# Spreading projection blocks over more steps of a two-branch attention kernel, and issuing its row transfers on two queues

## The chip, the cores and the metric

One core of one Trainium2 chip. The metric is device time in microseconds (us), the median of three runs. Engines: PE is TensorE, DVE is VectorE, ACT is ScalarE, POOL is GpSimd, SP is SyncE, which here only issues DMAs.

## What is computed

Two full self-attentions with weights of their own over the same input `x` of 2048 x 640, 32 heads of 20 features each, mixed by a gate per row. The input `B_x` takes no part.

```python
def attention(x, wqkv, wo):                      # for A and for B
    qkv = (x @ wqkv).reshape(B, S, 3, H, Dh).transpose(2, 0, 3, 1, 4)
    q, k, v = qkv[0], qkv[1], qkv[2]
    scores = einsum("bhqd,bhkd->bhqk", q, k) * Dh ** -0.5
    o = einsum("bhqk,bhkd->bhqd", softmax(scores), v)
    return o.transpose(0, 2, 1, 3).reshape(B, S, D) @ wo

g = sigmoid((x * gate_w).sum(-1, keepdims=True))
return g * attention(x, A_wqkv, A_wo) + (1 - g) * attention(x, B_wqkv, B_wo)
```

## The kernel before

The 64 heads of A and B are taken in 16 groups of four. A group's work is 4 row blocks of 512 queries, and each row block is 8 **steps** of 256 keys: 512 steps in all, numbered G, 32 to a group. "Step 5 of a group" counts from the group's first step, 0. The loop over G (L1121) writes the whole program in Python, engine by engine, before anything runs; the order on each engine is then fixed.

In every step stand

- the scores of the step: 8 products of 128 keys x 512 queries (`scores`, L631), each followed by an exponential on ACT (L642);
- the value products (`values`, L652) of the step before, which add into one bank, `acc`;
- 8 products for the row maxima (`max_mm`, L560) of a unit 14 or 15 steps ahead, each followed by a maximum over 512 keys on DVE (L587). In two of eight the pair goes another way, a relu on ACT (L580) and one operation of DVE (L584) that adds and takes the maximum at once. The first steps have up to 12 such products;
- none, one or two **blocks** of projection work (`X` in the lists `STEP`, L45). A block is a run of about 15 products (`mms`, L370) that fills a third of a chunk of Q and K features (`project_a`), of the rest of the Q features (`project_r`), a tile of V (`project_v`), or a part of the output projection (`products`, L710, and `last_tiles`, L820); then ACT drains it (L404, L532, L722).

An **empty** step has no block, a **single** one block, a **double** two. Score products use half of the rows of the TensorE array each, so the two heads of a pair run side by side. All these products and blocks write to a ring of seven PSUM banks.

Which blocks run where is planned in the list `fill`, with entries of a release step, a due step, a number of blocks and a generator (L1006, L1019, L1026). `behind` (L1062) adds up what is due; the loop (L1133) writes two blocks where `behind` says so, one where anything has been released, none otherwise. Other tasks are put at fixed steps with `at` and `tasks`: the load and split of the weights of the next groups (`weights_a`, `weights_r`, `weights_v`), the latter with a maximum and a scale on DVE (L511 to L513).

A projected chunk of Q and K lies in a tile `cq` (two halves of 1024 columns, each with a buffer), with features as rows. Before a group can use it, its rows must be **spread** (`spread`, L428) to the two pairs of heads in the tiles `kt` and `qt`, by 18 DMAs per half, and 4 for the differences of keys (`kd`, L469). Each `rows` call (L419) issues two DMAs, L423 and L425. In the steps all are issued by SP; in the start, before step 0, SP and POOL take turns. `later` (L485) waits for the second step of the group before and for the rest rows, then issues both halves, one DMA each time that the generators are advanced, eight times in a step. `spread_done` holds the halves that are out; maxima of a group are not written before its halves are in it.

After a unit's maxima are complete, `finish_max` (L591) transposes them, POOL casts them to `m4r`, and SP sends them through DRAM into rows of `qt` (L613, L617). At the end of a row block `take_acc` (L739) drains `acc`, makes the reciprocal sums with DVE and POOL (`sq`, `sh`) and sends the normalised rows to DRAM.

Of the kernel before, what the change touches and what calls it, by code (L numbers as in the profile page):

```python
# [24 lines left out]
NT = S // P  # L25
NC = D // P
GH = 4
NG = H // GH
GF = GH * DH
QB = 512  # L30
NQ = S // QB
NS = 8
STEPS = 2 * NG * NQ * NS
LEAD = 15
VW = DH + 1
XE = 7
QKS = 2.0 ** -12
# [25 lines left out]
def kernel(  # L63
# [10 lines left out]
    nc = tc.nc  # L74
# [47 lines left out]
    now = [-1]  # L122
# [153 lines left out]
    side = []  # L276
# [43 lines left out]
    spread_done = set()  # L320
    r_done, v_done = set(), set()
    rk = {}
# [26 lines left out]
    def rest_tiles(i):  # L349
        rk[i] = wts.tile([P, 2, S], F16, name="rk", tag="rk", bufs=1)  # L350

    def weights_r(i):

        st = {}

        def load():
            t = st["t"] = wts.tile([P, NC, 160], F32, name="wstage", tag="wstage", bufs=2)
            w = wqkv[i // 2].rearrange("(c p) f -> p c f", p=P)
            for j in range(4):
                f = (4 * (i % 2) + j) * GF + 48  # L360
                nc.sync.dma_start(t[:, :, 32 * j:32 * j + 32], w[:, :, f:f + 32])

        def split():
            hi, lo = blk["r", i] = block_tiles("r")
            rest_tiles(i)
            split_weights(st["t"][:, :, :P], r_qk[i][:, 0:1], hi, lo)

        return load, split
# [77 lines left out]
                yield from rows(qt[:, 1, cols], base, 8 * (1 - j), rk[g // 4][f, :, cols], 12 + 8 * j, False, queues)  # L446

    def project_r(i, ch):
        n = slice(ch * QB, (ch + 1) * QB)
        yield from project_chunk(blk["r", i], rk[i][:, 0, n], rk[i][:, 1, n], ch)  # L450
        r_done.add((i, ch))
# [24 lines left out]
    def project_a(g, ch):  # L476
        if ch % 2 == 0:
            half_tiles(g)
        hl = blk["q", g]
        n = slice((ch % 2) * QB, (ch % 2 + 1) * QB)  # L480
        yield from project_chunk(blk["a", g], hl[:, 0, n], hl[:, 1, n], ch)
        if ch == 1:
            key_differences(g, hl, work.tile([P, QB], F32, name="fs"), work.tile([P, 2, QB], F16, name="dd", bufs=1))
        if ch % 2 == 1:
            def later():  # L485
                for _ in range(10):
                    yield
                while not {(g // 4, c) for c in (ch - 1, ch)} <= r_done or now[0] < (g - 1) * NQ * NS + 1:
                    yield
                if ch == 1:  # L490
                    yield from spread_differences(g)
                yield from spread(g, hl, ch // 2 * 1024, 1024)
                spread_done.add((g, ch // 2))

            side.append(later())
# [494 lines left out]
    def at(G, f):  # L990
        todo.setdefault(G, []).append(f)

    def soon(due, blocks, gen):

        fill.append((0, due, blocks, gen))

    def tasks(G, gap, fs):
        for k, f in enumerate(fs):
            at(G + k * gap, f)

    at(4, sigmoids)
    for g in range(2 * NG):
        b = g * NQ * NS
        n = g + 1
        if n < 2 * NG:
            fill += [(b - 8, b + 4 + ch, 3, project_a(n, ch)) for ch in range(4)]  # L1006
            if n + 1 < 2 * NG:
                tasks(b + 15, 3, weights_a(n + 1))
            i = g // 4 + 1
            if i < 4:  # L1010
                if g % 4 == 0:
                    z, c0 = i // 2, 320 * (i % 2)
                    parts = max_tasks([[(wqkv[z], part * D + c0 + 160 * k) for k in range(2)] for part in range(2)],
                                      lambda m, i=i: scales_qk(i, m))
                    tasks(b + 2, 2, parts)
                if g % 4 == 2:
                    tasks(b + 18, 3, weights_r(i))
                if g % 4 == 3:
                    fill += [(b - 9, b + 4 + ch, 3, project_r(i, ch)) for ch in range(4)]  # L1019
# [51 lines left out]
    def slot(G):  # L1071
        if not current:
            able = [f for f in fill if f[0] <= G]
            if not able:
                return
            first = min(able, key=lambda f: f[1])
# [44 lines left out]
    for G in range(STEPS + 1):  # L1121
        g, qb, i = unit_of(G)
        now[0] = G
        while G < STEPS and ((g, qb) not in ready or (G and not valued(G - 1))):
            for u, ch in next_maxima(G, 1):
                for j in (1, 0):
                    one_max(u, ch, j)
            finish_step()
            advance()
            product()  # L1130
            slot(G)
        some = next_maxima(G, 4)
        blocks = 0 if not current and not any(f[0] <= G for f in fill) else 2 if behind(G) else 1  # L1133
        count = {}
        for what in (STEP[blocks] if maxima or some else LATE + " X" * (blocks == 2)).split():
            k = count[what] = count.get(what, 0) + 1
            if what[0] == "e":
                q = sum(count.get(f"e{j}", 0) for j in range(2)) - 1
                j = int(what[1])
                if G < STEPS:  # L1140
                    scores(G, (k - 1) // 2, (k - 1) % 2, (j,))
                finish_step()
                advance()
                if q == 3:
                    for f in todo.pop(G, []):
                        f()
                    out_tasks(G)
            elif what[0] == "m":
                for u, ch in some[(k - 1) * len(some) // 4:k * len(some) // 4]:
                    one_max(u, ch, int(what[1]))  # L1150
            elif what == "V":
                product()
                if G:
                    values(G - 1, k - 1)
                    if G % NS == 0 and k == 2 and G < STEPS:
                        side.append(take_acc(*unit_of(G - 1)[:2]))
                        advance()
            else:
                slot(G)
# [35 lines left out]
```

## Time and profile before

| | us |
|---|---|
| median of 3 runs (lowest, highest) | 2866.06 (2865.85, 2867.37) |
| the profiled execution | 2865.34 |
| its span, first to last instruction | 2863.5 |
| first exponential of step 0 | 97.7 |
| PE, ACT, DVE, POOL busy | 2805.2, 2567.4, 2405.1, 678.5 |

A row of a group names line, engine, operation, what is written from what, and the count; then the busy time and the mean in ns of one; then the idle time of the engine ahead of them and what ended most of it. A row of a stretch names its begin and end in us from the span's start, its length, each engine's busy time with the number of instructions in it, the granted clock as a share, the DMA engines' busy share and GB/s. In rows of one line's DMAs, `SPq` are the issues by SP, with the time of an issue as lowest/median/highest in ns. A wait row names who waited, for whom, the sum in us, how often, and the longest. PE's busy time counts products that overlap, so that it is near 100% whether or not PE is the limit; the length of a stretch says more.

### The profile page before, as it was taken

What the parts mean: (1) busy time and instruction counts of PE and PEld (TensorE: products, weight loads), DVE (VectorE), ACT (ScalarE), POOL (GpSimd) and SP (SyncE); (2) the same over time, 40 slices, a digit from 0 to 9 for tenths busy, and PEclk for the clock granted to TensorE, in tenths of its full rate; (3) what the DMA queues carried; (4) which work ended last, traced back from release to release, by engine and by line L of the source; (5) the groups of instructions that cost most, each with busy time, mean ns of one, the idle gap of its engine ahead of it and who ended that gap; (6) DMA issues with size and microseconds to landing.
All of it is one profiled execution on the core that took longest, in us unless ns stands there. A gap on an engine that the chain in (4) does not pass through costs nothing.

```text
span 2863.5 us, 63124 instructions
## 1 busy us (share of the span) xinstructions
PE 2805.2 (98%) x23489; PEld 982.2 (34%) x23489; DVE 2405.1 (84%) x4637; ACT 2567.4 (90%) x5249; POOL 678.5 (24%) x1103
## 2 busy tenths in 40 slices
PE   6999999999999999999999999999999999999998
PEld 3533223342323323343233333334433333332222
DVE  6688898878898898978988888887788888889982
ACT  3799999989999999989999999998899999888987
POOL 5322113221221212233431111322112233120011
PEclk9999999999999999999999999999999999999999
DMA  4110101001020101202022020210202112221222
GB/s 134 41 38 6 37 10 41 15 15 31 14 52 17 31 15 27 50 10 52 18 45 53 14 60 16 47 37 21 47 21 54 44 35 66 62 72 52 69 61 74
DMA packets 176761, 114.77 MB, mean 40 GB/s; under 512 B 111812, under 2 KB 150396, under 8 KB 176452
## 3 DMA queue, kind: packets, MB, share of 16 engines
q1 hardware_dynamic: 173908, 109.12, 15.9%
q8 instruction: 184, 3.01, 0.4%
q0 software_dynamic: 1600, 0.96, 0.2%
q14 instruction: 125, 1.02, 0.1%
q10 hardware_dynamic: 944, 0.66, 0.1%
HBM read 48.89 MB, written 26.61 MB: 26 GB/s over the span
## 4 chain that ended last, share of the span: by engine, by line
PE 91%; DVE 3%; ACT 2%; DMA 1%; issue 1%; POOL 1%; SPq 0%; POOLq 0%; ACTq 0%; DVEq 0%
PE acc L657 34%; PE bank L639 19%; PE bank L377 19%; PE bank L576 17%; DVE mpart L587 2%; ACT pt L642 1%; PE bank L763 1%; ACT rl L580 1%; PE bank L600 0%; DMA xs<-in_A_x_dram 0%; DMA wv<-in_A_wqkv_dram 0%; DVE rl L584 0%; PE bank L185 0%; ACT ot L742 0%; PE bank L880 0%
## 5 line engine op out<-in xcount | busy, mean ns | idle before, releaser
L642 ACT ACTIVATE pt<-bank 128x512 f32<-128x512 f32 x4096 | 2179.1, 613 | 154.5 <-PE bank L639 85.6
L587 DVE TENSOR_REDUCE mpart<-bank 128x1 f32<-128x512 f32 x2976 | 1883.8, 684 | 337.4 <-PE bank L576 202.8
L657 PE MATMUL acc<-pt,v 128*21 128x512 f32 x8192 | 1081.8, 600 | 2.5 <-ACT ot L742 2.4
L639 PE MATMUL bank<-qt,kt 64*128 64x512 f16 x4096 | 1054.7, 380 | 7.2 <-ACT pt L642 2.9
L576 PE MATMUL bank<-kt,qt 60*128 60x512 f16 x3536 | 1011.0, 380 | 4.6 <-DVE mpart L584 0.9
L576 PEld LDWEIGHTS <-qt 60*128 60x128 f16 x4096 | 235.2, 94 | 679.3 <-issue 621.6
L639 PEld LDWEIGHTS <-kt 64*128 64x128 f16 x4096 | 248.8, 94 | 461.6 <-issue 329.1
L584 DVE CUSTOM_DVE_ANT_0 rl<-bank,rl 128x512 f32<-128x512 f32 x560 | 378.6, 680 | 23.0 <-PE bank L576 9.2
L580 ACT ACTIVATE rl<-bank 128x512 f32<-128x512 f32 x560 | 332.8, 600 | 13.7 <-PE bank L576 11.4
L377 PE MATMUL bank<-xx,wbh 128*128 128x168 f16 (+2 forms) x2240 | 280.0, 244 | 4.5 <-ACT xx L884 1.9
L657 PEld LDWEIGHTS acc<-pt,v 128*21 128x21 f32 x8192 | 143.1, 99 | 403.8 <-issue 384.3
L377 PE MATMUL bank<-xx,wbl 128*128 128x168 f16 (+2 forms) x1120 | 253.0, 243 | 0.0
L768 POOL CAST on<-ot 128x512 f16<-128x512 f32 x63 | 38.5, 611 | 822.6 <-DVE ot L765 796.0
L377 PEld LDWEIGHTS <-wbh 128*128 128x128 f16 x2240 | 184.2, 98 | 87.4 <-issue 80.5
L576 PE MATMUL bank<-kd,qt 60*128 60x512 f16 x560 | 203.5, 381 | 1.6 <-DMA kd<-dd 1.2
L377 PE MATMUL bank<-wvh,xx 128*128 128x160 f16 (+1 forms) x1280 | 155.4, 234 | 0.5 <-ACT rl L580 0.2
L377 PE MATMUL bank<-woh,o_in 128*128 128x160 f16 (+1 forms) x960 | 155.7, 256 | 0.0
L377 PEld LDWEIGHTS <-xx 128*128 128x128 f16 x1920 | 131.9, 97 | 52.2 <-issue 49.0
L377 PE MATMUL bank<-wvl,xx 128*128 128x160 f16 (+1 forms) x640 | 137.3, 231 | 0.6 <-POOL wvl L317 0.6
L608 POOL CAST m4r<-mt 16x128 f16<-16x128 f32 x128 | 33.4, 284 | 437.8 <-ACT mt L605 437.8
L377 PEld LDWEIGHTS <-o_in 128*128 128x128 f16 (+1 forms) x1440 | 104.0, 97 | 75.3 <-issue 62.0
L404 ACT ACTIVATE fs<-bank 128x168 f32<-128x168 f32 (+1 forms) x216 | 69.3, 321 | 52.4 <-PE bank L377 38.7
(137 smaller groups left out, 1395.5 us busy)
## 6 DMA issues: line engine op xcount, KB each, us to landing
y_scr<-y_out SPq DMA_DIRECT2D x32, 320.0 KB
kt<-cq SPq DMA_DIRECT2D x120, 80.0 KB
o_scr<-on SPq DMA_DIRECT2D x240, 40.0 KB
kt<-cq SPq DMA_DIRECT2D x136, 40.0 KB
xs<-in_A_x_dram SPq DMA_DIRECT2D x8, 640.0 KB
o_in<-o_scr SPq DMA_DIRECT2D x32, 160.0 KB
y_out<-y_scr SPq DMA_DIRECT2D x16, 320.0 KB
xx<-y_scr SPq DMA_DIRECT2D x16, 320.0 KB
```

Of the source, the lines that this page charges most:

```text
L377: nc.tensor.matmul(out_ap, a, b, start=(k == 0), stop=(k == len(pairs) - 1))
L404: nc.scalar.activation(f[:, m], pt[:, m], AF.Copy, scale=QKS)
L576: nc.tensor.matmul(pt, QT[g % 2][r, pair, q0:q0 + P], k, start=True, stop=True)
L580: nc.scalar.activation(relus[u, j], pt, AF.Relu)
L584: nc.vector.tensor_tensor_reduce(rl, pt, rl, 1.0, LOW, OP.add, OP.max, m)
L587: nc.vector.tensor_reduce(m, pt, axis=AX.X, op=OP.max)
L608: nc.gpsimd.tensor_copy(m4[:, k, :], mt)
L639: nc.tensor.matmul(et, KT[g % 2][r, pair, kt * P:(kt + 1) * P], QT[g % 2][r, pair, qb * QB:(qb + 1) * QB], start=True, stop=True)
L642: nc.scalar.activation(pt, et, AF.Exp, scale=factor(g // 4))
L657: nc.tensor.matmul(acc[32 * h:32 * h + VW, :], V[(g // 2) % 2][:, kt, (g % 2) * GH + h, :], ptiles.pop((G, kk, h)), start=(kt == 0), stop= ...
L763: nc.tensor.matmul(pt, sel.rearrange("k h e -> k (h e)"), sr, start=True, stop=True)
L768: nc.gpsimd.tensor_copy(o[:, 0], ot)
```

## The change

Blocks: `blocks_of` takes the place of the rule "two if behind, else one". A credit grows by `MEAN`, 0.72 a step in A's half and 1.1 in B's, and is spent by the blocks written; a step gets one when the credit has reached 1 or when the work would be behind at a rate of 0.8 blocks a step, and two when it is behind at a rate of 1. The release and due steps of all projections are moved, and weights are loaded and split earlier: `weights_a` by 3 steps, `weights_r` by 2, `weights_v` by 8 (but for the first). The tile of the rest rows, `rk`, is taken at its first block, not with its weights. Blocks of Q and K carry a fifth entry, and may not begin before that half of the group before has been spread.

Rows: in the steps, SP and POOL now take turns in a spread, so L423 stays with SP and L425 goes to POOL. The second half waits for step 8 of the group before instead of step 1, and for the first half.

```diff
+MEAN = (0.72, 1.1)
...
     def project_r(i, ch):
+        if i not in rk:
+            rest_tiles(i)
...
             def later():
+                two = cycle((nc.sync, nc.gpsimd))
                 for _ in range(10):
                     yield
-                while not {(g // 4, c) for c in (ch - 1, ch)} <= r_done or now[0] < (g - 1) * NQ * NS + 1:
+                while (not {(g // 4, c) for c in (ch - 1, ch)} <= r_done or now[0] < (g - 1) * NQ * NS + (1, 8)[ch // 2]
+                       or ch == 3 and (g, 0) not in spread_done):
                     yield
                 if ch == 1:
-                    yield from spread_differences(g)
-                yield from spread(g, hl, ch // 2 * 1024, 1024)
+                    yield from spread_differences(g, two)
+                yield from spread(g, hl, ch // 2 * 1024, 1024, queues=two)
...
+    def able(G):
+        return [f for f in fill if f[0] <= G and (f[4] is None or f[4][0] == 0 or f[4] in spread_done)]
...
-            fill += [(b - 8, b + 4 + ch, 3, project_a(n, ch)) for ch in range(4)]
+            fill += [(b - 13, b + (1, 3, 6, 8)[ch] + 3 * (g % 4 == 3), 3, project_a(n, ch), (n - 1, ch // 2)) for ch in range(4)]
             if n + 1 < 2 * NG:
-                tasks(b + 15, 3, weights_a(n + 1))
+                tasks(b + 12, 3, weights_a(n + 1))
...
                 if g % 4 == 2:
-                    tasks(b + 18, 3, weights_r(i))
+                    tasks(b + 16, 3, weights_r(i))
                 if g % 4 == 3:
-                    fill += [(b - 9, b + 4 + ch, 3, project_r(i, ch)) for ch in range(4)]
+                    fill += [(b - 12, b + 2 * ch, 3, project_r(i, ch), (g, 1)) for ch in range(4)]
...
-                at(b, load)
-                at(b + 3, lambda scale=scale: side.append(scale()))
-                at(b + 7, split)
-                fill += [(b + 10, b + 14 + 3 * j, 2, project_v(gg, j)) for j in range(0, NT, 2)]
+                b0 = b - 8 if g else b
+                at(b0, load)
+                at(b0 + 3, lambda scale=scale: side.append(scale()))
+                at(b0 + 7, split)
+                fill += [(b0 + 10, b0 + 18 + 2.9 * j, 2, project_v(gg, j), None) for j in range(0, NT, 2)]
...
-    def behind(G):
+    def behind(G, rate):
         n = sum(f[0] for f in current)
-        for f in sorted((f for f in fill if f[0] <= G), key=lambda f: f[1]):
+        for f in sorted(able(G), key=lambda f: f[1]):
             n += f[2]
-            if n > max(1, f[1] - G):
+            if n > max(1, rate * (f[1] - G)):
                 return True
         return False
+    credit = [0.0]
+    def blocks_of(G):
+        if not current and not able(G):
+            return 0
+        credit[0] = min(max(credit[0], -1.0) + MEAN[G >= NG * NQ * NS], 2.0)
+        n = 2 if behind(G, 1.0) else max(int(behind(G, 0.8)), int(max(credit[0], 0.0)))
+        credit[0] -= n
+        return n
...
-        blocks = 0 if not current and not any(f[0] <= G for f in fill) else 2 if behind(G) else 1
+        blocks = blocks_of(G)
```

The lines of the kernel after stand up to nineteen further down than those before; L580, L642 and L532 of before are L584, L646 and L536, and L404 is L404 in both.

ACT's order shows the blocks best, since each has one drain. In group 1, at the step that begins with 42, ACT before has exponentials and a relu only:

```order
L642 ACTIVATE pt<-bank_93 128x512
L642 ACTIVATE pt<-bank_89 128x512
L642 ACTIVATE pt<-bank_92 128x512
L580 ACTIVATE rl<-bank_90 128x512
L642 ACTIVATE pt<-bank_94 128x512
```

At the same place after, the drain of a V tile has come in between:

```order
L646 ACTIVATE pt<-bank_89 128x512
L646 ACTIVATE pt<-bank_90 128x512
L536 ACTIVATE v_87<-bank_94 128x8x20
L646 ACTIVATE pt<-bank_91 128x512
L584 ACTIVATE rl<-bank_89 128x512
```

A block of V has moved into an empty step; steps 40 and 43 got one too, and 41 stays empty. In group 2, where step 89 begins, ACT before drains two blocks of a chunk, the end of one step's and the beginning of the next's:

```order
L642 ACTIVATE pt<-bank_94 128x512
L642 ACTIVATE pt<-bank_89 128x512
L404 ACTIVATE fs<-bank_90 128x168
L404 ACTIVATE fs<-bank_91 128x168
L580 ACTIVATE rl<-bank_92 128x512
L642 ACTIVATE pt<-bank_93 128x512
```

After, it drains one:

```order
L646 ACTIVATE pt<-bank_89 128x512
L646 ACTIVATE pt<-bank_93 128x512
L404 ACTIVATE fs<-bank_92 128x168
L646 ACTIVATE pt<-bank_94 128x512
L584 ACTIVATE rl<-bank_91 128x512
```

The second block of this step has gone to an earlier one. On POOL, at the beginning of group 2, before, the casts of the negated maxima (`m4r`) and of the reciprocals (`sh`) follow each other with a chunk's casts between:

```order
L558 MEMSET mpart 128x2x4
L608 CAST m4r<-mt 16x128 x2
L610 TENSOR_TENSOR m4r<-mt,m4r 16x128 x2
L406 CAST cq<-fs 128x512
L407 TENSOR_TENSOR cq<-fs,cq 128x512
L752 TENSOR_SCALAR sq<-sq 128x16
L753 CAST sh<-sq 128x16
```

After, transfers of the spread stand among them:

```order
L562 MEMSET mpart 128x2x4
L425 DMA qt_81<-cq 20x1024
L425 DMA qt_81<-cq 8x1024
L425 DMA qt_81<-rk 12x1024
L612 CAST m4r<-mt 16x128 x2
L614 TENSOR_TENSOR m4r<-mt,m4r 16x128 x2
L425 DMA kt_83<-cq 20x1024 x2
L425 DMA qt_81<-cq 20x1024
L425 DMA qt_81<-rk 20x1024
L756 TENSOR_SCALAR sq<-sq 128x16
L757 CAST sh<-sq 128x16
```

What POOL does here for the maxima and the reciprocals now stands behind the issue of DMAs, and behind what these wait for.

More of the change, by code (lines that the diff above doesn't have):

```diff
@@ L364, in split @@
             hi, lo = blk["r", i] = block_tiles("r")
-            rest_tiles(i)
             split_weights(st["t"][:, :, :P], r_qk[i][:, 0:1], hi, lo)
@@ L993, in soon @@
     def soon(due, blocks, gen):
-        fill.append((0, due, blocks, gen))
+        fill.append((0, due, blocks, gen, None))
+    def able(G):
+        return [f for f in fill if f[0] <= G and (f[4] is None or f[4][0] == 0 or f[4] in spread_done)]
     def tasks(G, gap, fs):
@@ L1060, in out_tasks @@
             soon(now[0] + 6, 4, last_tiles(*last.pop(0)))
-    def behind(G):
+    def behind(G, rate):
         n = sum(f[0] for f in current)
-        for f in sorted((f for f in fill if f[0] <= G), key=lambda f: f[1]):
+        for f in sorted(able(G), key=lambda f: f[1]):
             n += f[2]
-            if n > max(1, f[1] - G):
+            if n > max(1, rate * (f[1] - G)):
                 return True
         return False
+    credit = [0.0]
[6 more added lines that the diff above has]
+        return n
     def slot(G):
         if not current:
-            able = [f for f in fill if f[0] <= G]
-            if not able:
+            if not able(G):
                 return
-            first = min(able, key=lambda f: f[1])
+            first = min(able(G), key=lambda f: f[1])
             fill.remove(first)
```

## The prediction

> **What bounds the kernel now.** I read the busy shares and the chain first, then the groups, then stretches of eight steps cut out of the steady part, because an average over stages with different limits says little here.
>
> ```profile
> PE 2805.2 (98%) x23489; PEld 982.2 (34%) x23489; DVE 2405.1 (84%) x4637; ACT 2567.4 (90%) x5249; POOL 678.5 (24%) x1103
> ...
> PE 91%; DVE 3%; ACT 2%; DMA 1%; issue 1%; POOL 1%; SPq 0%; POOLq 0%; ACTq 0%; DVEq 0%
> PE acc L657 34%; PE bank L639 19%; PE bank L377 19%; PE bank L576 17%; DVE mpart L587 2%; ACT pt L642 1%; PE bank L763 1%; ACT rl L580 1%; PE bank L600 0%; DMA xs<-in_A_x_dram 0%; DMA wv<-in_A_wqkv_dram 0%; DVE rl L584 0%; PE bank L185 0%; ACT ot L742 0%; PE bank L880 0%
> ```
>
> TensorE carries 91% of the chain, and the blocks (L377) are 19% of it. That looks like a kernel in which only TensorE's work counts. The stretches say otherwise. Each row below is exactly eight steps of 32-step groups after the ramp, so its length over eight is the price of a step. In order: all empty (steps 40 to 47), all with one block (360 to 367), the same at another place (56 to 63), all with two blocks (88 to 95), one empty step among singles (368 to 375), three empty ones, of which one stands alone and two together (304 to 311), one double among singles (312 to 319).
>
> ```profile
> core 0: us, PE busy (x) PEld busy (x) DVE busy (x) ACT busy (x) POOL busy (x), PEclk, DMA share, GB/s
> 332.70:370.68 37.98, 37.32 (x262) 8.74 (x258) 35.91 (x68) 36.95 (x75) 3.80 (x10) 1.00 0.10 19
> 409.48:452.01 42.53, 42.53 (x380) 15.27 (x378) 36.03 (x67) 39.88 (x83) 12.53 (x19) 1.00 0.08 19
> 2042.48:2084.66 42.18, 42.18 (x380) 14.89 (x378) 36.06 (x67) 39.96 (x82) 5.58 (x12) 1.00 0.19 43
> 577.92:629.47 51.55, 51.30 (x499) 24.17 (x498) 36.79 (x68) 42.39 (x91) 17.82 (x25) 1.00 0.04 8
> 2084.66:2126.41 41.75, 41.75 (x367) 14.17 (x363) 36.09 (x68) 39.49 (x82) 8.38 (x16) 1.00 0.10 23
> 1727.40:1768.38 40.98, 40.54 (x337) 12.66 (x333) 36.00 (x68) 38.97 (x79) 8.39 (x16) 1.00 0.10 22
> 1768.38:1811.74 43.36, 43.36 (x395) 16.14 (x393) 36.13 (x67) 40.42 (x83) 5.57 (x12) 1.00 0.09 23
> ```
>
> The reader should see VectorE's 36 us in every row. In the empty stretch it is 35.91 of 37.98: the row maxima hold the step, and TensorE has room that nobody uses. In the double stretch VectorE idles for 15 us and TensorE alone holds the step. So the first block in a step is cheap, (42.18 - 37.98) / 8 = 0.53 us, and the second is dear, (51.55 - 42.53) / 8 = 1.13 us. Moving a block from a double step to an empty one should give 0.6 us.
>
> **The order.** I counted the blocks that each step holds in TensorE's order of both programs. All 512 steps and the tail hold 471 blocks in both. From step 14 to 496, where every step has eight maxima, before has 103 empty steps and 51 doubles, after has 91 and 42. Before, only 7 empties and 6 doubles stand alone; the others follow one another, up to 18 empties and 16 doubles. After, 58 empties and 23 doubles stand alone. So the change converts only about ten pairs; what it really does is to break up the runs, and the sum depends on what a step standing alone is worth.
>
> An empty step alone: the stretch with one of them in eighth place gives 42.18 - 41.75 = 0.43. In the stretch with three, taking 0.53 each for the two that stand together, the one in second place gives 42.18 - 40.98 - 1.06 = 0.14. Places 2 to 4 hold the closing work of a row block, and 20 of the 58 fall there, so I take (38 x 0.43 + 20 x 0.14) / 58 = 0.33. The bounds are 0.14 and 0.53. The reason I see for less than 0.53: the order is fixed and a seven-bank ring lets TensorE run ahead by less than half of a step's sixteen score and maxima products, so a single hole is only partly usable.
>
> A double alone: 43.36 - 42.53 = 0.83. One row only; the bounds are that and 1.13.
>
> - Empties, saving before: 7 x 0.33 + 96 x 0.53 = 53.2; after: 58 x 0.33 + 33 x 0.53 = 36.6. The change loses **16.6 us**.
> - Doubles, cost before: 6 x 0.83 + 45 x 1.13 = 55.8; after: 23 x 0.83 + 19 x 1.13 = 40.6. It wins **15.2 us**.
>
> **The ramp.** Steps 0 to 13 hold 16 blocks before and 14 after; the two go into later steps and are in the counts above.
>
> ```profile
> 97.71:194.78 97.07, 92.18 (x722) 36.43 (x722) 79.51 (x182) 81.33 (x170) 20.48 (x29) 0.98 0.20 48
> ```
>
> These steps take 6.9 us each, with 10 to 12 maxima in most of them, so a block here costs between nothing and 1.13. I take 0.5 each, a win of **1.0 us**. From step 497 to the end both hold 24 blocks: nothing.
>
> **The V weights.** Six of seven loads, with their maximum and scale on VectorE, move eight steps ahead.
>
> ```profile
> 452.01:493.33 41.32, 40.76 (x316) 11.47 (x312) 37.84 (x79) 38.03 (x78) 12.08 (x17) 1.00 0.26 54
> 963.56:1004.02 40.46, 40.43 (x341) 12.50 (x337) 35.73 (x67) 38.56 (x80) 7.28 (x14) 1.00 0.25 53
> 1811.74:1855.54 43.80, 43.53 (x385) 15.85 (x383) 38.18 (x79) 40.12 (x83) 18.99 (x24) 1.00 0.24 50
> 2343.57:2385.86 42.29, 42.29 (x380) 15.05 (x378) 36.01 (x67) 39.90 (x82) 26.27 (x26) 1.00 0.32 73
> ```
>
> Steps 64 to 71 hold four empties and the scaling, steps 160 to 167 two empties and none: 41.32 - 40.46 + 2 x 0.53 = 1.92 us for the scaling beside empties. Steps 320 to 327 and 416 to 423, all singles, with and without: 43.80 - 42.29 = 1.51. Four of the six stood beside empties and move to mostly single steps: 4 x 0.41, say a win of **1.5 us**. The bounds are nothing and 4 x 1.92 = 7.7.
>
> **The two queues.** Every second transfer of a spread, L425, goes from SP to POOL: 120 + 90 + 60 + 30 = 300 issues.
>
> ```profile
> L425 SPq DMA_DIRECT2D kt<-cq x120: 723/740/1292, 129.4 to 2561.2; - x120
> L425 SPq DMA_DIRECT2D qt<-cq x90: 659/729/1503, 132.6 to 2562.8; - x90
> L425 SPq DMA_DIRECT2D qt<-rk x60: 723/748/984, 135.7 to 2564.4; - x60
> L425 SPq DMA_DIRECT2D kd<-dd x30: 724/745/793, 126.2 to 2523.4; - x30
> L425 POOL DMA_DIRECT2D kt<-cq x16: 507/507/619, 39.7 to 60.1; - x16
> DMA to landing us min/median/max: 1.6/1.8/3.0
> ```
> ```profile
> PE bank L576 <- DMA kd<-dd: 1.2, 1, 1.2
> PE bank L377 <- POOL wvl L317: 0.6, 1, 0.6
> ACT fs L404 <- POOL cq L407: 1.9, 1, 1.9
> ```
>
> SP loses 300 x 0.74 = 222 us of issuing and POOL gains 300 x 0.507 = 152 us on top of 678.5. Neither is a gain by itself: all that TensorE waited for a spread is the 1.2 us of the first row, so that is the most that a faster spread can give. The second half of a spread now goes out at steps 8 to 10 of a group instead of 4 to 6 (in groups 4, 8 and 12 to 13), and its first reader is the maximum at step 18: 5 to 8 steps, 26 us or more, against a landing of 1.8. On POOL, behind the issues, stand the casts of the negated maxima (`m4r`), the reciprocal's halves (`sh`) and the blocks' casts. With 22 issues in three steps a cast comes at most 22 x 0.507 = 11 us late; the row maxima are asked for 16 us after they have been sent (issue of the last at 476.9 in step 68, their step 72 begins at 493.3), and the two short waits for POOL above are all that the parts waited. Without that cover each of 15 groups would pay up to 11 us. I take nothing.
>
> The Trainium skill (DMA: Bandwidth & Descriptors, "Issuing engines are not separate DMA queues") says that starting transfers on several engines saves only the sequencer's time, usually small beside the transfer. Here the issue, 0.74 us, is not small beside a landing of 1.8, so the trace bears out only the first half; by the rule the term is zero, by the row it is zero too, since the saved 222 us are not waited for.
>
> **New waits.** The rest rows' weights are split at step 83 instead of 85 of the third group, and their first block comes at step 84 instead of 89.
>
> ```profile
> L307 POOL TENSOR_SCALAR wstage<-wstage,r_qk 128x640 f32<-128x640 f32 x3 | 5.7, 1884 | 0.0
> L310 POOL TENSOR_TENSOR wbl<-wstage,wbh 128x640 f16<-128x640 f32 x3 | 4.2, 1406 | 0.3
> L308 POOL CAST wbh<-wstage 128x640 f16<-128x640 f32 x3 | 2.2, 718 | 0.2
> ```
>
> That is 1.88 + 0.72 + 1.41 = 4.0 us of POOL behind the casts at the end of step 82, against 5.2 us of step 83: it fits with a microsecond to spare. If it does not, TensorE and all behind it stand for up to 4 us, three times, 12 us. I take nothing. The waits for `spread_done` in the table of blocks hold nothing back: the spread is done at step 10 to 13 of a group and the blocks that ask for it come free from step 19.
>
> **Sum:** +16.6 - 15.2 - 1.0 - 1.5 = -1.1 us. The profiled execution took 2865.34 (span 2863.5); that gives 2864.2, and the median of the runs shown lies 0.7 above it: **2865**. A measurement of this kernel can tell about 0.2%, 5.7 us, from no change; this is none.
>
> **Rivals.**
>
> *A lone empty step is worth as much as one in a run* (it buys 0.53). For it: the row with 0.43; the blocks are then spread as the words of the change say. Against it: the 0.14. Time: 51 more lone empties x 0.20 = 10 us less, **2855**.
>
> *Lone empties are wasted and lone doubles are not cheap.* The ring cannot carry TensorE's spare time past one step: an empty buys 0.14 and a double costs 1.13 wherever it stands. For it: the second-place row, and that the price of a lone double rests on one stretch. Against it: 0.43 and 0.83. It costs 51 x 0.19 + 17 x 0.30 = 15 us, **2880**. With doubles at 0.83, it decides from a lone empty under 0.20: then the time is over 5.7 us longer.
>
> *The split or POOL's casts come late*, after all: up to 12 us at three places, **2877**; it shows as TensorE waiting for POOL at L377.
>
> *POOL's issues are stretched beside VectorE.* At the longest POOL issue shown, 0.62, 22 of them last 14 us, still inside the 16. The Trainium skill (SBUF — State Buffer, "SBUF: two separate sides") warns that VectorE in a two-port mode keeps GpSimd from writing descriptors. No issue above shows that. If each took twice 0.62, the casts would come 27 us late, 11 beyond the cover, in 15 groups: 165 us, **3030**.
>
> *The change does not do what it says.* It does, barely: from step 14 to 496 a block runs in 392 steps instead of 380. Were the lone steps worth what they are in runs, that alone would be the first rival; nothing else of it is left.
>
> **How the numbers follow.** No change, 2865, 43%; wins as in a run, 2855, 26%; wasted empties, 2880, 22%; late split, 2877, 8%; stretched issues, 1%. The likeliest case's own range is 2859 to 2871; the range takes in the two neighbours, 2850 to 2882. Faster by over 0.2% 0.26, within 0.43, slower 0.31.
>
> **What would show it.** A stretch of eight steps with three lone empties among singles should cost 42.18 - 3 x 0.33 = 41.2; 40.6 speaks for the first rival, 41.8 for the second. TensorE should show no wait for POOL or a DMA of `kt` over 2 us in total. Step lengths should come in three close kinds as above, with no single step over 7 us outside the ramp. A ramp (97.7 to 194.8 before) that differs by more than 3 us, a wait on L377 at step 84, or POOL issues over 0.6 us would make the prediction wrong.

## The result and the profile after

The kernel after takes 2870.14 us (median of 20 runs, 2869.0 to 2872.43), the kernel before, beside it on the same chip, 2866.35 (20 runs, 2865.29 to 2868.15). The ratio is 1.0013, with the interval 1.0006 to 1.002: slower, by less than the 0.2% that was taken as the line of no change. Forecast were 2865 and a change of -1.1; measured is +3.8. The size is small, but where it comes from is not where any step of the prediction looked.

The profiled execution of after took 2870.04 (span 2868.2), 4.70 more than that of before. First the busy shares and the chain of after, as the page has them:

```profile
PE 2801.2 (98%) x23489; PEld 976.0 (34%) x23489; DVE 2402.9 (84%) x4637; ACT 2567.3 (90%) x5249; POOL 829.9 (29%) x1403
...
PE 90%; DVE 3%; ACT 3%; POOL 1%; DMA 1%; issue 1%; SPq 0%; POOLq 0%; DVEq 0%; ACTq 0%
```

POOL has 300 instructions and 151 us more, as forecast, and all else reads as before. Nothing here tells of 4.7 us: a share of the chain under half of one per cent prints as 0%, and 0.3% is what is looked for. So the span has to be cut. The next rows are stretches of before, then of after: steps 0 to 13, steps 14 to 496, steps 497 to 510.

```profile
97.71:194.81 97.10, 92.21 (x722) 36.43 (x722) 79.51 (x182) 81.36 (x171) 20.48 (x29) 0.98 0.20 48
194.81:2778.00 2583.19, 2565.77 (x21689) 876.82 (x21685) 2237.75 (x4276) 2375.42 (x4849) 590.37 (x961) 1.00 0.16 36
2778.00:2840.92 62.92, 62.02 (x460) 17.00 (x461) 18.50 (x37) 57.61 (x116) 6.74 (x15) 1.00 0.20 60
```
```profile
98.38:193.57 95.19, 90.31 (x692) 33.91 (x692) 79.17 (x182) 81.01 (x168) 35.15 (x55) 0.98 0.20 48
193.57:2778.00 2584.43, 2563.98 (x21718) 873.94 (x21715) 2235.91 (x4276) 2375.78 (x4850) 727.12 (x1235) 1.00 0.15 36
2778.00:2840.98 62.98, 62.08 (x460) 16.99 (x461) 18.51 (x37) 57.61 (x116) 6.74 (x15) 1.00 0.19 60
```

Before step 0: +0.67 (98.38 - 97.71). Steps 0 to 13: -1.91. Steps 14 to 496: +1.24. Steps 497 to 510: +0.06. Step 511 begins at 2840.92 in both within 0.06. What is left is the end: 2863.5 - 2840.92 = 22.6 us before, 2868.2 - 2840.98 = 27.2 after. **The whole loss, 4.6 us, lies behind the beginning of the last step.** POOL's last row there, before and then after, is the last addition of the output, and it comes at the same time in both:

```profile
2857.84 0.86 POOL L835 TENSOR_TENSOR xx<-xx,pt 128x320 f32<-128x320 f32 x1 [1.05 <-ACT pt L834]
```
```profile
2857.83 0.86 POOL L839 TENSOR_TENSOR xx<-xx,pt 128x320 f32<-128x320 f32 x1 [1.05 <-ACT pt L838]
```

So the computation ends together. Behind it stand only the DRAINs with which each engine closes the program. A row gives lowest/median/highest time in ns, then the first and the last start; the highest of POOLq is the one that begins while the last addition still runs. Before, then after:

```profile
L1190 POOLq DRAIN  x3: 34/102/4911, 2857.8 to 2863.3; - x3
L1190 SPq DRAIN  x3: 7/7/7, 2861.7 to 2863.0; - x3
```
```profile
L1209 POOLq DRAIN  x3: 34/102/9647, 2857.8 to 2868.0; - x3
L1209 SPq DRAIN  x3: 7/7/7, 2861.1 to 2867.7; - x3
```

SP's first drain, behind the last stores, stands at 2861.7 and 2861.1. POOL's lasts 4911 ns before and 9647 ns after: 2858.70 is the end of the last addition, 2857.8 + 4.91 = 2862.7 the end of the drain before (4.02 us behind the addition, to the unrounded start), 2857.8 + 9.65 = 2867.5 that of after (8.75 behind it). The difference is 4.74 us, and that of the two spans is 4.73 (the medians of the runs differ by 3.8). It is no wait for transfers under way: POOL's last transfer in after is issued at 2568.3, some 290 us earlier, and in before POOL issues none behind the start.

Below, "the drain" is this time from POOL's last operation to the end of its DRAIN.

### The profile page after: what moved, and what is told of

Same layout as the page of the kernel before. It is cut to its first block, busy times and chain, and to the rows that moved or that the text cites. A ratio compares the mean times of both kernels' runs of the same rounds, so it can differ in the third digit from the quotient of the medians.

```text
span 2868.2 us, 63192 instructions
## 1 busy us (share of the span) xinstructions
PE 2801.2 (98%) x23489; PEld 976.0 (34%) x23489; DVE 2402.9 (84%) x4637; ACT 2567.3 (90%) x5249; POOL 829.9 (29%) x1403
## 3 DMA queue, kind: packets, MB, share of 16 engines
q0 software_dynamic: 11200, 11.43, 1.7%
q14 instruction: 125, 1.02, 0.1%
## 4 chain that ended last, share of the span: by engine, by line
PE 90%; DVE 3%; ACT 3%; POOL 1%; DMA 1%; issue 1%; SPq 0%; POOLq 0%; DVEq 0%; ACTq 0%
PE acc L661 33%; PE bank L377 19%; PE bank L643 18%; PE bank L580 17%; DVE mpart L591 2%; ACT pt L646 2%; PE bank L767 1%; ACT rl L584 1%; PE bank L604 0%; DMA xs<-in_A_x_dram 0%; DMA wv<-in_A_wqkv_dram 0%; ACT ot L746 0%; PE bank L186 0%; DVE rl L588 0%; PE bank L835 0%
## 5 line engine op out<-in xcount | busy, mean ns | idle before, releaser
L646 ACT ACTIVATE pt<-bank 128x512 f32<-128x512 f32 x4096 | 2179.3, 613 | 154.5 <-PE bank L643 87.5
L580 PE MATMUL bank<-kt,qt 60*128 60x512 f16 x3536 | 1015.8, 380 | 4.0 <-DVE mpart L591 0.5
L580 PEld LDWEIGHTS <-qt 60*128 60x128 f16 x4096 | 234.6, 94 | 709.4 <-issue 654.6
L584 ACT ACTIVATE rl<-bank 128x512 f32<-128x512 f32 x560 | 333.3, 600 | 13.2 <-PE bank L580 11.3
L377 PE MATMUL bank<-xx,wbh 128*128 128x168 f16 (+2 forms) x2240 | 281.8, 244 | 2.7 <-ACT xx L888 1.9
L377 PE MATMUL bank<-xx,wbl 128*128 128x168 f16 (+2 forms) x1120 | 253.0, 243 | 1.5 <-POOL wbl L311 1.5
L377 PEld LDWEIGHTS <-wbh 128*128 128x128 f16 x2240 | 182.6, 98 | 95.4 <-issue 87.1
L580 PE MATMUL bank<-kd,qt 60*128 60x512 f16 x560 | 203.7, 380 | 1.3 <-DMA kd<-dd 1.2
L406 POOL CAST cq<-fs 128x512 f16<-128x512 f32 x60 | 36.7, 612 | 412.0 <-ACT fs L404 409.9
L377 PE MATMUL bank<-woh,o_in 128*128 128x160 f16 (+1 forms) x960 | 155.7, 256 | 0.2 <-ACT pt L646 0.2
L377 PE MATMUL bank<-wvh,xx 128*128 128x160 f16 (+1 forms) x1280 | 154.8, 234 | 0.4 <-ACT rl L584 0.2
L377 PEld LDWEIGHTS <-xx 128*128 128x128 f16 x1920 | 132.0, 97 | 49.2 <-issue 46.2
L377 PE MATMUL bank<-wvl,xx 128*128 128x160 f16 (+1 forms) x640 | 137.2, 231 | 0.6 <-POOL wvl L318 0.6
L377 PEld LDWEIGHTS <-o_in 128*128 128x128 f16 (+1 forms) x1440 | 104.0, 97 | 75.4 <-issue 63.1
```

The costliest lines, as they stand in the source:

```text
L377: nc.tensor.matmul(out_ap, a, b, start=(k == 0), stop=(k == len(pairs) - 1))
L406: nc.gpsimd.tensor_copy(hi, f)
L580: nc.tensor.matmul(pt, QT[g % 2][r, pair, q0:q0 + P], k, start=True, stop=True)
L584: nc.scalar.activation(relus[u, j], pt, AF.Relu)
L646: nc.scalar.activation(pt, et, AF.Exp, scale=factor(g // 4))
```

## The experiments

Theory 1: POOL's closing drain depends on the transfers that POOL has issued, 48 before (all in the start) and 348 after, and everything else in the change cancels. Rival 2: the schedule of blocks loses the 4 us, and the drain only waits for something else that is late. Rival 3: the bytes that POOL moves, or how late it moves them, set the drain.

| kernel | us (median) | ratio to before | drain, us | POOL transfers |
|---|---|---|---|---|
| only SP issues, rest as after | 2866.12 | 0.9997 [0.9988, 1.0006] | 4.02 | 48 |
| two queues alone, rest as before | 2871.25 | 1.0018 [1.0009, 1.0027] | 8.75 | 348 |
| after, last additions on VectorE | 2865.6 | 0.9996 [0.9987, 1.0005] | 8.75 | 348 |
| before and 300 tiny transfers | 2870.6 | 1.0017 [1.0008, 1.0027] | 8.75 | 348 |
| before, POOL issues nothing | 2892.78 | 1.009 [1.0074, 1.0105] | 0.07 | 0 |
| after, without the running mean | 2855.99 | 0.9964 [0.995, 0.9978] | 8.75 | 348 |
| the three edits together | 2849.95 | 0.9941 [0.9927, 0.9954] | 4.02 | 48 |
| after, second halves on SP alone | 2869.6 | 1.001 [1.0, 1.0019] | 7.61 | 213 |
| before and 80, 396, 500, 1000 tiny | 2871.26, 2868.43, 2868.5, 2878.63 | one run each, no interval | 10.55, 6.71, 5.32, 6.63 | 128, 444, 548, 1048 |

### Only SP issues

```diff
-                two = cycle((nc.sync, nc.gpsimd))
+                two = repeat(nc.sync)
```

> The kernel after with all transfers of a spread on SP again; blocks, waits and release steps stay. Theory, the closing drain of POOL: it grows with the number of transfers that POOL issued (4.91 us with 48, 9.65 with 348), so with 48 it is 4.9 again, and the time falls by 4.7 to about 2865.4; the 512 steps stay within 1.5 us. Rival, the order: the 3.8 us are in the steps and the drain hides behind the last output transfer; then the time stays at 2870 or rises, because SP issues 300 more transfers.

Measured: 2866.12. With the new order of blocks and all transfers on SP the kernel is level with before, and the drain is again that of before:

```profile
L1209 POOLq DRAIN  x3: 34/102/4911, 2859.5 to 2864.9; - x3
```

Steps 14 to 496 take 2584.1 us with one queue (the row below) and 2584.4 with two.

```profile
194.16:2778.28 2584.12, 2564.00 (x21718) 873.91 (x21715) 2235.91 (x4276) 2375.77 (x4850) 585.95 (x955) 1.00 0.15 36
```

The schedule's share of the change is therefore nothing that can be measured, and rival 2 falls.

### Two queues alone

```diff
+                two = cycle((nc.sync, nc.gpsimd))
-                    yield from spread_differences(g)
-                yield from spread(g, hl, ch // 2 * 1024, 1024)
+                    yield from spread_differences(g, two)
+                yield from spread(g, hl, ch // 2 * 1024, 1024, queues=two)
```

> The kernel before with one change: SP and POOL take turns in the spreads of the steps (300 transfers go to POOL). Theory, the closing drain: the steps keep their length within 1 us, the drain is 9.6 us, and the time is 2866.35 + 4.7 = 2871. Rival, the order: the queues cost nothing, 2866; or POOL's casts come late, and then the steps grow, not the end.

Measured: 2871.25, and the long drain with the order of blocks of before. The two queues alone give the whole loss.

```profile
L1191 POOLq DRAIN  x3: 34/102/9646, 2856.8 to 2866.9; - x3
```

### Last additions on VectorE

The last three half rows' additions, POOL's last work, go to VectorE; POOL is done some six us earlier.

```diff
-                if half and qb == NQ - 1 and t < 3:
+                if False:
```

> The kernel after; the last three halves of rows are added by VectorE straight from the bank, not by ScalarE and POOL, so that POOL's last work ends 5 us sooner. Theory, the closing drain: it begins when POOL's own last work is done (at 2853.5 instead of 2858.7), so its 8.8 us run beside the last sums and output transfers and end near 2862.3; the time falls by 4 to 5 us, less up to 1 us if VectorE is late: about 2865.5. Rival: the drain waits for all engines, or its length is not POOL's: 2870.

Measured: 2865.6, level with before again.

```profile
L1209 POOLq DRAIN  x3: 34/102/9776, 2851.5 to 2861.8; - x3
L1209 SPq DRAIN  x3: 7/7/7, 2859.2 to 2861.5; - x3
```

The drain is as long as in after (8.75 us from POOL's last operation, at 2852.53), but it begins six us earlier, so most of it lies beside the last work of the other engines. It waits for nothing that is late: its length follows POOL's own end. It still ends about 2 us behind SP's (2851.5 + 9.78 = 2861.3 against 2859.2), so not all of it is hidden.

### Tiny transfers

To the kernel before come 300 transfers of 32 bytes from POOL to a scrap tile in DRAM, one in each of steps 100 to 399; nothing waits for them.

```diff
+                    if 100 <= G < 400:
+                        nc.gpsimd.dma_start(junk[G - 100:G - 99, :], ident[0:1, 0:8])
```

> The kernel before with 300 transfers of 32 bytes added on POOL, one in each of steps 100 to 399, from a constant to a scratch of DRAM that nothing reads. Theory, number of transfers: POOL's drain ends 8.75 us after its last work, as with the 300 spread transfers of 17 KB to 82 KB, and the time is 2866.5 + 4.7 = 2871.2. Rival, bytes or the spreads themselves: the drain ends 4.0 us after the last work, as before, and the time is 2866.5.

Measured: 2870.6. The drain is that of after to 3 ns, with 0.99 MB on POOL's queue in place of 11.43 MB, other bytes, and no transfer behind step 399:

```profile
L1193 POOLq DRAIN  x3: 34/102/9644, 2857.9 to 2868.1; - x3
```
```profile
q0 software_dynamic: 11200, 0.99, 0.3%
```

Rival 3 falls with this: at this number of transfers, neither the bytes nor the steps in which they are issued matter. The number of packets on that queue, 11200, is the same as in after.

### POOL issues nothing

The 48 transfers of the start go from POOL to ACT.

```diff
-            nc.gpsimd.dma_start(KT[i][64 * j + 60:64 * j + 64], mrow.unsqueeze(1).to_broadcast([4, 2, S]))
+            nc.scalar.dma_start(KT[i][64 * j + 60:64 * j + 64], mrow.unsqueeze(1).to_broadcast([4, 2, S]))
...
-    both = cycle((nc.sync, nc.gpsimd))
+    both = cycle((nc.sync, nc.scalar))
```

> The kernel before with no transfer on POOL: the 48 of the start go to ScalarE's queue. Theory, number of transfers, on the line through 48 and 348 (4.02 and 8.75 us after POOL's last work): 4.02 - 48 x 0.0158 = 3.26 us, 0.8 us less at the end; the start may be up to 2 us longer, since ScalarE issues between its drains of the first blocks. Rival: a part of the drain is there only once POOL has issued any transfer; then it falls by more, up to 4 us.

Measured: 2892.78, for another reason. The drain is gone, where theory 1's straight line left 3.26 us of it; the recorded rival, that a part is there only once POOL has issued any transfer, is the one that came:

```profile
L1190 POOLq DRAIN  x3: 39/82/957, 2888.8 to 2892.7; - x3
L1190 SPq DRAIN  x3: 7/7/7, 2892.1 to 2892.4; - x3
```

But step 0 begins at 127.88 in place of 97.71, 30.2 us later, where at most 2 were expected:

```profile
127.88:224.73 96.85, 91.98 (x722) 36.21 (x722) 79.50 (x182) 81.34 (x170) 20.44 (x29) 0.98 0.20 48
224.73:2807.88 2583.15, 2565.32 (x21689) 877.25 (x21685) 2237.03 (x4276) 2375.39 (x4849) 588.88 (x961) 1.00 0.15 36
```
```profile
L425 ACTq DMA_DIRECT2D kt<-cq x16: 727/728/856, 42.0 to 70.7; - x16
```

44 issues of 0.73 us are 32 us on ACT, which in the start also copies the features that the next issues send. Of the chain over the first 128 us they are 13.5%, 17 us; the other 13 us were not taken apart. The steps are those of before. ACT's own DRAINs, now behind 48 issues, stay at 150 ns at most, as in before. The end gained only 0.5 us (22.6 to 22.1), since SP's drain at 2892.1 and a last operation 1.1 us later take its place: of before's 4.02 us of drain, three lay beside the last stores (2861.7 - 2858.7). A drain begins to cost from there on, where SP closes.

### Without the running mean

The release and due steps, the waits and the two queues stay; only the rule of blocks is again "two if behind, else one".

```diff
-        n = 2 if behind(G, 1.0) else max(int(behind(G, 0.8)), int(max(credit[0], 0.0)))
+        n = 2 if behind(G, 1.0) else 1
```

> The kernel after without the running mean: one block wherever one may run, two when behind; release and due steps and both queues stay. From step 14 to 496 the order then has 78 empty steps (6 alone, 72 in runs) and 26 doubles, against 91 (58 alone) and 42. Theory, prices by step: an empty alone saves 0.33 and in a run 0.53, a double costs 1.13, so the steps are 21.6 us shorter than after (6 x 0.33 + 72 x 0.53 = 40.1 less 26 x 1.13 = 29.4, against 36.6 less 47.5), the ramp with two more blocks 1 us longer, the drain stays at 9.6: about 2849.5. Rival, only the sum of TensorE's work counts, which is the same: 2870.

Measured: 2855.99, 14.15 below after, with after's drain. This order has 78 empty steps (6 alone) and 26 doubles (4 alone) between steps 14 and 496; after has 91 (58) and 42 (23, of which one, step 462, has the order of a double but holds one block). Of group 3, steps 96 to 127, the blocks of each step:

```
after              11111111102001011001011011101101
without the mean   11111111111000000001111111111110
```

Both write 23 blocks. The rows of this group, after first:

```profile
625.95:794.46 168.51, 166.13 (x1386) 54.56 (x1382) 146.15 (x281) 156.09 (x320) 55.87 (x93) 1.00 0.11 24
```
```profile
624.25:790.12 165.87, 165.01 (x1375) 53.29 (x1371) 145.90 (x280) 155.80 (x318) 59.03 (x95) 1.00 0.11 24
...
195.00:2763.34 2568.34, 2554.11 (x21692) 868.94 (x21690) 2235.86 (x4277) 2376.94 (x4849) 726.36 (x1235) 1.00 0.15 36
```

Ten holes in pieces and one double cost 2.6 us more than nine in runs (eight, and one that the next group carries on) and none. Over steps 14 to 496 it is 2584.4 - 2568.3 = 16.1. Here the recorded expectation was too high (21.6), because it charged the lone doubles of after 1.13 instead of the prediction's 0.83. By the prediction's own prices: after, 36.6 won by empties - 40.6 paid for doubles = -4.0; this order, 6 x 0.33 + 72 x 0.53 = 40.1, less 4 x 0.83 + 22 x 1.13 = 28.2, is +11.9; the difference is 15.9 against 16.1.

### The three edits together

Without the mean, SP alone, and the last additions on VectorE (the three diffs above, on after).

> The kernel after without the running mean, with all transfers of a spread on SP, and the last three adds on VectorE. Theory: the steps of the kernel without the mean (2856.0), less the 4.7 us of the drain, less about 1 us for the drain that then ends before the last output transfer: 2850. Rival, that SP's load or the queues carried part of that kernel's gain in the steps: 2853 or more.

Measured: 2849.95, 0.9941 of before [0.9927, 0.9954]; it is the fastest kernel here, and below after by 20.2. Its steps 14 to 496 take 2568.4, and POOL is done before SP:

```profile
L1209 POOLq DRAIN  x3: 34/102/5036, 2838.6 to 2847.9; - x3
L1209 SPq DRAIN  x3: 7/7/7, 2847.3 to 2847.7; - x3
```

The drain ends at 2838.6 + 5.0 = 2843.7 and costs nothing.

### How the drain grows: second halves on SP

The rest of the runs ask what the drain's length is made of. Here POOL issues in first halves only, 213 transfers.

```diff
-                yield from spread(g, hl, ch // 2 * 1024, 1024, queues=two)
+                yield from spread(g, hl, ch // 2 * 1024, 1024, queues=two if ch == 1 else repeat(nc.sync))
```

> The kernel after with only the first half of each spread and the key differences on both queues: 11 transfers a group, 165 in 15 groups, go to POOL, 213 in all. Theory, so much for every transfer: the drain ends 4.02 + 165 x 0.0158 = 6.6 us after POOL's last work, and the time is 2.1 us below after, 2868. Rival, a step from few to many transfers: 4.0 or 8.75 us, and 2865.4 or 2870.

Measured: 2869.6, with a drain of 7.61 us. A straight line through 48 and 348 gives 4.02 + 165/300 x 4.73 = 6.6, so the line falls; the rival, a step from the one value to the other, falls as well.

```profile
L1209 POOLq DRAIN  x3: 34/102/8501, 2858.3 to 2867.4; - x3
```

### How the drain grows: 80, 500, 1000 and 396 tiny transfers

Before, with so many tiny transfers from step 0 on (one a step; two a step for 1000), one run each.

```diff
+                    for k in range(1 if G < 80 else 0):
+                        nc.gpsimd.dma_start(junk[1 * G + k:1 * G + k + 1, :], ident[0:1, 0:8])
```

> The kernel before with 80 transfers of 32 bytes added on POOL, one in each of steps 0 to 79; nothing reads them. Four counts have shown 0.07 us (0), 4.02 (48), 7.61 (213) and 8.75 (348) between POOL's last work and the end of its drain. Theory, a cost that grows ever more slowly with the count (2.4 us for each factor of e): with 128 in all 4.02 + 2.4 x ln(128 / 48) = 6.4 us. Rival, straight pieces between the counts shown: 4.02 + 80 x 0.0218 = 5.8 us.

> The kernel before with 500 transfers of 32 bytes added on POOL, one in each of steps 0 to 499. Theory, growth that slows down: with 548 in all 8.75 + 2.4 x ln(548 / 348) = 9.8 us from POOL's last work to the end of its drain. Rivals: 8.75 + 200 x 0.0084 = 10.4 on the straight line of the last two counts; or 8.75, a limit.

> The kernel before with 1000 transfers of 32 bytes added on POOL, two in each of steps 0 to 499. Theory, growth that slows down: with 1048 in all 8.75 + 2.4 x ln(1048 / 348) = 11.4 us from POOL's last work to the end of its drain. Rivals: 8.75 + 700 x 0.0084 = 14.6 on the straight line of the last two counts; or 8.75, a limit.

> The kernel before with 396 transfers of 32 bytes from POOL in steps 0 to 395 (one each), 444 POOL transfers in all. The drain after POOL's last operation so far, against this number: 48 gives 4.02 us, 128 10.55, 213 7.61, 348 8.75, 548 5.32, 1048 6.63. Theory A (the drain hangs on the place within a ring of 64: 48, 548 and 1048 lie at 50, 38 and 26 with the two that start the program counted, and fall on one line of 0.109 us a place): 446 lies at 62, so about 2.7 us, and POOL's drain ends before SP's own closing drain; the end is some 1.3 us nearer than in the kernel before, about 2865 in all. Theory B (a base that grows by 2.6 ns a transfer, 4.02 to 5.32 to 6.63, and something besides that the counts in between add): at least 5.0 us, about 2867 or more. Theory C (it lies between its neighbours 348 and 548): 5.3 to 8.8 us, 2867 to 2871.

Measured, in the order 80, 500, 1000, 396:

```profile
L1193 POOLq DRAIN  x3: 34/102/11442, 2857.0 to 2869.0; - x3
```
```profile
L1193 POOLq DRAIN  x3: 34/102/6214, 2859.7 to 2866.4; - x3
```
```profile
L1193 POOLq DRAIN  x3: 34/102/7524, 2868.5 to 2876.5; - x3
```
```profile
L1193 POOLq DRAIN  x3: 34/102/7602, 2858.2 to 2866.3; - x3
```

The drain does not grow with the count. 128 transfers give the longest, 10.55 us, and 548 a short one, 5.32. The straight line, slowing growth and a limit of 8.75 fall with the first three. A place in a ring of 64, which the times of 48, 548 and 1048 suggested, asked for 2.7 us at 444, and 6.71 came: it falls too. The other two theories of that run, a slow base with something added or a value between the neighbours, are both met, and tell nothing apart. **What sets the length beside the number of transfers stays open.** Settled is that no transfers give no drain, that five kernels with 348 give 8.75 whatever the size, the bytes and the step, and that three kernels with 48 give 4.02. With the 1000 transfers the steps take 8 us longer, too (2591.4 against 2583.2); why was not looked into.

## Why the prediction was right and wrong

**The step that failed** is "The two queues", with its words "I take nothing", and beside it "From step 497 to the end both hold 24 blocks: nothing". Both weighed only what runs in the steps: issues, casts behind them, readers. The end was costed by its blocks, though before's own rows showed POOL's drain of 4911 ns there, reaching a microsecond past SP's. The size could not be had from that row, but it would have made a rival: a drain that depends on what POOL issues. Measured is +4.7 us (4.02 to 8.75); it vanishes with SP alone, comes with the queues alone, comes with 300 unrelated tiny transfers, and is hidden where POOL ends earlier. The rule that the prediction cites (the Trainium skill, DMA: Bandwidth & Descriptors, "Issuing engines are not separate DMA queues"), that issuing on several engines saves only the sequencer's time, agrees with the runs as far as it goes: the steps gained nothing (2584.1 with one queue, 2584.4 with two).

**Empties and doubles** were right in their sum. The forecast was +16.6 - 15.2 = +1.4 for steps 14 to 496, measured +1.2, and the same prices give the order without the mean within 0.4 us, against either kernel. The count of after is one double too high: at step 462 TensorE has the order of a double, but no products between the last scores of that step and the first of the next; and 14 blocks in the ramp, 434 and 24 would make 472, not 471. With 41 doubles the forecast is +0.5, and the order without the mean is off by 1.1 against after. Stretches of after, in order: steps 44 to 51 and 64 to 71, three lone empties each; 120 to 127 and 152 to 159, two lone empties each, the first with a load's maximum and scale; 384 to 391, a lone double:

```profile
351.48:392.25 40.77, 40.36 (x335) 12.77 (x333) 35.86 (x67) 38.77 (x79) 8.40 (x16) 1.00 0.05 11
455.40:496.61 41.21, 41.09 (x348) 13.54 (x344) 36.10 (x69) 39.24 (x82) 11.56 (x24) 1.00 0.20 44
751.23:794.46 43.23, 42.51 (x357) 14.29 (x353) 38.19 (x80) 39.30 (x81) 15.81 (x22) 1.00 0.04 8
920.66:962.05 41.39, 41.36 (x350) 13.56 (x348) 35.98 (x67) 38.92 (x80) 12.49 (x19) 1.00 0.04 8
2171.97:2215.30 43.33, 43.33 (x397) 16.08 (x393) 36.12 (x68) 40.34 (x83) 13.36 (x26) 1.00 0.20 47
```

Three lone empties were to cost 41.2: 40.77 and 41.21. Two: 42.18 - 0.66 = 41.5, measured 41.39. The double: 43.36 forecast, 43.33. The two main rivals, 0.53 and 0.14 for a lone empty, both lose by the total, which either would have put 10 or 15 us away.

The single prices are less sure than this looks, because the result depends on which singles a stretch is held against. The prediction names its two rows of singles in the wrong order (the first, 42.53, is steps 56 to 63 in A's half, the second, 42.18, is 360 to 367 in B's), and it took the lone double of steps 312 to 319, in B's half, from the 42.53 of A's; from 42.18 it costs 1.18, not 0.83. In after, eight singles cost 42.60 in A's half (steps 88 to 95, the next row), from which the lone empties above save 0.46 to 0.61.

```profile
583.35:625.95 42.60, 42.60 (x380) 15.28 (x378) 36.06 (x67) 39.82 (x83) 7.34 (x14) 1.00 0.03 7
```

Whole groups with the same loads are a better test. Groups 1 and 12, after first, then without the mean:

```profile
288.69:455.40 166.71, 164.89 (x1375) 53.24 (x1371) 145.70 (x280) 155.84 (x319) 48.57 (x84) 1.00 0.11 24
2171.97:2346.26 174.29, 173.97 (x1564) 64.20 (x1562) 149.35 (x288) 160.82 (x331) 51.42 (x86) 1.00 0.16 40
```
```profile
292.58:455.39 162.81, 161.35 (x1300) 49.02 (x1296) 145.76 (x280) 154.09 (x314) 46.80 (x82) 1.00 0.11 24
2158.82:2331.07 172.25, 171.92 (x1534) 62.02 (x1532) 149.18 (x288) 160.20 (x329) 51.32 (x86) 1.00 0.17 41
```

In group 1, 14 empties in runs stand against 9 alone: a lone one is worth (14 x 0.53 - 3.90) / 9 = 0.39. In group 12, one lone double stands against three: each costs 2.04 / 2 = 1.02. With these two prices and 41 doubles the forecast is +0.4: the lone double was priced too low and the lone empty a little too low, and in the sum the two nearly cancel. That part is luck.

**The V weights** were mis-sized: -1.5 forecast. Steps 120 to 127 and 152 to 159 have the same blocks, and with the scaling cost 43.23 - 41.39 = 1.84 more. By this one pair, the load at its new place costs what it did beside empties (1.92), not as little as at the singles (1.51), so the move gains nothing: at the new place the steps have holes too. With 0 for this term, empties and doubles alone (+0.5, or +1.4 by the prediction's count) stand against the measured +1.2.

**The ramp** was forecast at -1.0 and came to -1.9; the other kernels with that order of blocks took 93.8 to 95.4 in it (after 95.2), so a part of this is scatter.

**The start** is +0.67, in no step of the prediction. Between 97.6 and 99.1 us it scatters in all kernels that leave it alone; nothing is to be explained there.

**The waits** stayed small. The waits of TensorE in after:

```profile
PE bank L377 <- POOL wbl L311: 1.5, 2, 0.8
PE bank L580 <- DMA kd<-dd: 1.2, 1, 1.2
PE bank L377 <- POOL wvl L318: 0.6, 1, 0.6
```

That is 3.3 us in all against 1.8 for `kd` and `wvl` before. The split of the rest rows is late twice, at the first block of the rest rows (steps 84 and 212), by 0.8 us at most, not by 4; no `kt` is waited for. By the letter, three of the prediction's signs of being wrong came with this: a wait on L377 at step 84, 2.1 us of waits for POOL in all, and POOL issues over 0.6 us (before already had one of 619 ns). The waits for POOL are 2.1 us in all, and the loss lies elsewhere. POOL's issues beside VectorE keep their median length, so the stretched issues fall:

```profile
L425 POOL DMA_DIRECT2D kt<-cq x136: 507/515/625, 40.3 to 2567.3; - x136
```

The prediction also counted too many issues ahead of the casts: of the 22 of a first half every second one is SP's, so POOL issues 11 of them, which last 5.6 us and not 11.

Body and start together, -1.91 + 1.24 + 0.06 + 0.67 = +0.06, are as good as nothing; the drain is the change.

And where did the gain of the planner go? The moved release and due steps are worth 2583.2 - 2568.3 = 14.9 us in the steps (the order without the mean against before), with half the doubles (26 against 51) and most holes still in runs. The running mean takes 16.1 back: it holds blocks away from steps that could have had them, and its order has 16 more doubles by the count and its holes alone.

## What to carry to other kernels

Cost the end of a program by each engine's close, not by its work: here POOL, once it had issued transfers, closed 4 to 11 us behind its last operation. So let it finish its work early, or issue from SP, whose own DRAIN stayed at 7 ns. Price a step by a stretch of steps like it, alone and in a run, and against singles of the same part of the program: a hole that stands alone was worth about 0.3 to 0.4 us here and one in a run 0.53, so spreading work evenly can lose even where it removes doubles. And when a change moves little, undo its parts one at a time: here a gain of 14.9 lay under a loss of 16.1 and another of 4.7.

## What the runs showed of the hardware

- POOL's closing drain behind its last operation, by the number of transfers that POOL issued: 0.07 us (0), 4.02 (48), 10.55 (128), 7.61 (213), 8.75 (348), 6.71 (444), 5.32 (548), 6.63 (1048). It is the same to some ns in the three kernels with 48 and in the five with 348, with other sizes and other steps of issue; the law over the count is open. SP's own DRAIN stayed at 7 ns in all kernels, and ACT's at 150 ns at most with 48 transfers on ACT.
- With the start's 48 issues on ACT, 44 of them at 0.73 us, step 0 began 30.2 us later than with the same issues on POOL, at 0.51, where it began at 97.7.
